# A gated dilated convolution on TensorE: seventeen six-step groups and three more short four-step groups in another order, in place of eighteen six-step groups

## The chip, the cores and the metric

The kernel runs on one core of one Trainium2 chip. A core has engines that run side by side and wait for each other by semaphores: TensorE (PE in the profile; PEld is its weight load), VectorE (DVE), ScalarE (ACT), GpSimd (POOL) and SyncE (SP, which here only issues DMAs). Matmul results lie in PSUM, everything else in SBUF. The metric is the device time of one execution in microseconds (us); lower is better.

## The reference

x has 2 sequences of 16,000 steps with 256 channels. A causal convolution with three taps, two steps apart, makes 512 channels; the first half goes through tanh, the second through a sigmoid, their product through a 256 x 256 matrix.

```python
B, T, D, K = (2, 16000, 256, 3)
dil = 2; pad = (K - 1) * dil
xp = jnp.pad(x, ((0, 0), (pad, 0), (0, 0)))
h = jnp.einsum('btc,cd->btd', xp[:, pad:pad + T, :], w[0])
for i in range(1, K):
    off = pad - i * dil
    h = h + jnp.einsum('btc,cd->btd', xp[:, off:off + T, :], w[i])
f, g = h[..., :D], h[..., D:]
z = jnp.tanh(f) * _sigmoid(g)
return z @ w_o
```

All data are bf16.

## The kernel before

**Fewer multiplications.** Steps are handled in groups. A group of kind B takes 4R successive steps and lays four of them beside each other; four products with transformed weights and inputs (m, p, d0, d3) replace the six that the taps would need. A group of kind A takes 6R steps and needs five products (by u1, rm, rp, r0, ri) where nine would be needed. R is 256 unless the table GROUPS says otherwise (B160 has R = 160). The first 640 steps (P160) are computed directly, by `direct`. So a product of kind A or B is a matmul of 2R columns, done for both halves of the channels (CT = 2, so always a pair), and one *block* is a group's products for one of four slices of 128 output channels (`oi` = 0 to 3).

**What each engine does for a block.** `product` issues TensorE's pairs: F (first), M (mid, kind A only), L (last), Z (zero), I (inf). `copy_first` (token c) has ScalarE copy the first product from PSUM to `ss`. `combine` (A, Y) and `second` (h; k is the same on ScalarE) are VectorE's sums over PSUM, tiles `a`, `yy` and `hh`; `activate` (b, y, a) is ScalarE's tanh or sigmoid, tiles `th` and `sg`. A block of kind A needs three of these sums (`hh`, `a`, `yy`), one of kind B only `a`. When both halves of a group's channels are done, `gate` (g) multiplies them on VectorE into `zz`, `out_mm` (P; H and R for the last group) applies w_o, and ScalarE or VectorE (tokens e and v, `out_evict`) moves the result to `osb`, from where SP stores it (s). Leftovers of R beyond a multiple of 128 go through `zo` and `odd`.

**The inputs of the products.** SP loads x transposed into `xt` (`load`, token x). `pre` makes the transformed inputs. Each may be made by VectorE in one instruction (128x1024, `u1.4`), by GpSimd in four quarters (128x256, tokens with q, as `u2.4q74`: the number tells behind which earlier VectorE instruction the quarter is held), or, for the second half of rp, rm, r0 and ri, by a DMA that adds one tile onto another in SBUF, issued from GpSimd's queue (tokens with d; rp lies in tile f, rm in e, r0 in u0, ri in u2, and the profile calls u0 to u3 all `u`). u3, uh and ud are scalings of u1. Tokens `wa` make one weight matrix on GpSimd at the start.

**What sets the order.** Nothing is scheduled by the compiler: ORDER lists the blocks by group number, and PLAN is one long list of tokens, each of which issues one instruction (or one pair or set of four matmuls). All engines run their own instructions in the order of that list. A and B blocks take their PSUM from two pools (`ps_b` with three banks, `ps_a` with two), output matmuls from `ps_o` with three.

Of the kernel before, what the change touches and what calls it, by code (L numbers as in the profile page):

```python
# [21 lines left out]
m.0 d3.0 p.0 F F d0.0 c F c G L w L A c D wa.5q2 D A wa.2q5 Z d0.1 I b D m.1 a L wa.3q1 F d A wa.10q2 Z c p.1 I  # L22
wa.6q1 b L a G Z wa.14q10 F A b x wa.4q7 I c g P a d3.1 F L u1.0 c wa.0q1 Z A I b wa.13q1 P e.0 a Z f.0 F b P g I x
c uh.0 L e0 m.2 L d3.2q1 a F A e1 P d3.2q2 A c Z u0.0 I b I u3.0 a r0.0d Z u2.0 L p.2 b x d3.2q1 F e2 A P e3 F ud.0
c d0.2 Z a I u1.1 c L b g P d3.2q1 a L A e4 F wa.12q14 A Z wa.8q30 c e.1 I b Z g a L u1.2 b F wa.1q1 P e5 A ri.0d F
c rp.0 I e6 rm.0 L c s3 Z u3.1 a s2 M uh.1 s0 b uh.2 I x u2.1 k0 P a A F wa.7q1 e7 L u0.1 wa.9q11 P c A Z e8 wa.11q6
M ud.1 wa.15q28 b I Y k1 F f.1 a Z f.2 c I b L g x M a A F k2 u2.2 P u1.3q14 c L Y e9 M u1.3q54 A y I k3 rp.1d u3.2
P Y a Z L g e10 Z b A f.3q36 P y ud.2 F f.3q28 b Y P c r0.1d rm.1 P y Z ri.1d e.2 e11 F e.3 I b rm.2d M g c F k4 M
u0.2 u0.3q1 a L h5 c I y A f.3q12 L a M f.3q62 Y e12 P A u1.3q8 e13 Z I Y k6 u1.3q43 I b g ri.2d L a rp.2d F u3.3 y
Z A rm.3d c P u1.4 b r0.2d P a Y M rp.3d F y uh.3 Z ud.3 k7 v15 I b L u3.4 e14 ud.4 F f.4q68 c A P c M u0.3q20 Y a M  # L30
e.4 k8 Z k9 g L rm.4d b I u0.3q33 A e17 P a v16 F f.4q36 L y Y s8 P f.4q55 c x A Z y u2.4q74 M Y b I e18 h10 Z a F g
b P c L u2.3 F e19 u1.5 ri.3d M c A I u0.3q60 k11 M Y a L u0.4 y f.4q1 P A k12 I Z e20 r0.3d uh.4 Y P a rp.4d L b
f.5 r0.4d Z y A F b I g c P u2.5q72 y F Y M e21 u3.5 u2.5q4 I c v22 P y u2.4q90 h13 Z a u2.4q16 v23 M b L u2.4q50
h14 a s10 P s9 e24 u2.5q44 A F x y L Y e.5q82 P c A e.5q79 Z e25 Y M e.5q58 y I h15 b e.5q69 Z a g ri.4d F e26 L c I
A f.6q22 b P s11 uh.5 M a u2.5q82 Y F y rp.5d u0.5 P k16 Z e.6 e27 r0.5d L b g I c P u2.6q118 A y F M e28 u1.6q63 Y
P c f.6q1 h17 Z y I ud.5 e29 rm.5 M b s12 L h18 a u2.6q1 x F a P u2.6q45 A c L Y u1.6q20 e30 I A u1.6q108 e31 M Z a
Y u1.6q33 P k19 g ri.5d Z b L e32 u0.6 P f.7q89 y A I b F uh.6 u2.6q46 e33 P Y c F r0.6d u3.6 P y g rm.6d M e34 I
f.6q13 a h20 P c Z y u1.7 L f.6q67 b M A e35 P rp.6d Y F k21 s14 P a e.7 s13 Z c ud.6 I g e36 ri.6d L b M u2.7q71 A
e37 P a h22 F u0.7q137 e38 P Y u0.7q65 c L s15 Z y uh.7 x u2.7q72 A M b I f.7q90 h23 e39 F f.7q1 y Y L c f.7q114 I
v40 a Z u2.7q22 Y a M g P b P k24 A F e41 x L rp.7 e42 P c A Z y u1.8 I u0.8q93 b M Y a P u0.7q161 h25 Z y F uh.8 b  # L40
u3.7 I u2.8 s16 c rm.7d F e43 f.8 M c L g rp.8d k26 M a u2.7q76 A L k27 Y I y u0.8q1 A Z a u0.7q103 P v44 b u0.8q81
L Y y s17 P u0.8q162 A e45 F r0.7d e46 Z ud.7 Y c I ri.7d P b u3.8 r0.8d M u1.9 a Z e.8 k28 F b ud.8 L rm.8d e.9 c I
y g F u2.9q179 M y A P c P e47 h29 f.9q46 M a Y s18 f.9q43 L e48 s1 ri.8 u2.9q60 Z x k30 I A b L u2.9q117 Y a F y
# [23 lines left out]
uh.17 p.3q67 Z e103 A M p.3q36 b s37 ud.17 I m.3q10 k67 Y P u0.17q286 a F v106 p.3q135 y L r0.17d Z c A P u2.17q16 y
M Y b I u2.17q30 e105 h68 Z a v107 F ri.17q5 b L ri.17q4 s38 y I A ri.17q3 P c Y F y ri.17q28 M c g Z a P h69 b P g
e108 M L e109 h70 F y I A c P a Y L I y Y Z a A M b P h71 y Z v110 F b L c I A F a L Y P c A I e113 v111 Z a L v112
Z b P A b s40 I g y s39 P a F I v114 c F P g c L a Z e115 A L P v116 b I e117 A Z s41 P g a s6 I b v118 Z a P b P  # L70
e119 g H P v120 s42 R P e121 H e123 v122 H R s44 R e124 s43 e125 s45
"""


# [572 lines left out]
```

## Time and profile before

| what | value |
|---|---|
| median of 3 runs | 258.78 us (258.61 to 259.19) |
| the profiled execution's own time | 258.77 us |
| its span, first to last instruction | 256.6 us |
| granted TensorE clock, mean | 0.995 |
| GpSimd's accumulating DMAs | 64 (18 + 16 + 15 + 15), 256 KB each |

The profile is of one execution; its span leaves out 2.2 us around the first and last instruction. A row of a group has the source line, engine, operation, output and input tiles with their shapes, a count, then the busy time, the mean duration in ns, and idle time before it with what ended that. A row of stretches has, after the stretch, each engine's busy time with a count. In the chain of work that ended last each piece has its start and its length, both in us, and what was running. Instructions that follow each other on one engine overlap a little, so the distance from start to start is the price of one more, and is less than its duration.

### The profile page before, as it was taken

To read this page: it belongs to the slowest core of one execution; us is meant where nothing else is said; L and a number is where in the kernel's file an instruction comes from. 1 tells how busy PE (TensorE), PEld (TensorE's weight loads), DVE (VectorE), ACT (ScalarE), POOL (GpSimd) and SP (SyncE) were. 2 spreads that over 40 slices of the span, in tenths; PEclk is the share of its full clock that TensorE was granted. 3 is DMA by queue.
4 is the path that set the end of the run, shared out by engine and by line. 5 is a ranking of instruction groups with operands and counts; after the bars stand their busy time and mean duration, and the time that the engine had idled before them with its cause. 6 is when DMAs were issued, how large, how long until landed. Compare 5 with 4: busy or idle time off the path is not lost.

```text
span 256.6 us, 4575 instructions
## 1 busy us (share of the span) xinstructions
PE 249.9 (97%) x1428; PEld 138.0 (54%) x1428; DVE 242.8 (95%) x405; ACT 243.7 (95%) x492; POOL 176.9 (69%) x249
## 2 busy tenths in 40 slices
PE   8999999999999999999999999999999999999992
PEld 4655555555555565545555555555555545555581
DVE  2999999999999999999999999999999999999991
ACT  4988999999999999999999999999999999999893
POOL 1064554997699888499764887999798798897000
PEclk9999999999999999999999999999999999999997
DMA  6999979989989899999999999996999998773054
GB/s 184 213 202 213 196 172 159 232 143 203 187 199 271 187 200 249 182 289 200 200 237 212 249 196 188 290 244 147 212 260 171 216 219 224 198 217 102 0 226 176
DMA packets 84320, 51.73 MB, mean 202 GB/s; under 512 B 69032, under 2 KB 70312, under 8 KB 84296
## 3 DMA queue, kind: packets, MB, share of 16 engines
q1 hardware_dynamic: 74168, 33.71, 54.3%
q0 software_dynamic: 9216, 16.78, 37.7%
q10 hardware_dynamic: 912, 0.95, 1.1%
q8 instruction: 11, 0.18, 0.3%
q14 instruction: 13, 0.11, 0.1%
HBM read 1.25 MB, written 16.38 MB: 69 GB/s over the span
## 4 chain that ended last, share of the span: by engine, by line
PE 82%; DVE 8%; DMA 3%; ACT 2%; issue 2%; ACTq 0%; DVEq 0%
PE b L359 48%; PE o_ps L478 18%; PE a L359 13%; DVE a L393 2%; DMA e<-u 2%; DVE zz L460 2%; DVE yy L393 2%; PE b L379 1%; PE a L379 1%; DMA xn<-in_x_dram 1%; DVE hh L393 1%; ACT osb L495 1%; ACT sg L441 1%; ACT th L441 0%; ACT ss L390 0%
## 5 line engine op out<-in xcount | busy, mean ns | idle before, releaser
L330 POOL TENSOR_TENSOR u<-xt 128x256 bf16<-128x256 bf16 x88 | 66.8, 774 | 15.0 <-PE b L359 8.4
L478 PE MATMUL o_ps<-wo_sb,zz 128*128 128x256 bf16 x496 | 72.0, 273 | 0.0
L495 ACT CAST osb<-o_ps 128x512 bf16<-128x512 f32 x101 | 63.8, 646 | 0.9 <-PE o_ps L478 0.7
L478 PEld LDWEIGHTS <-zz 128*128 128x128 bf16 x496 | 48.5, 98 | 27.6
L393 DVE SCALAR_TENSOR_TENSOR a<-ss,b 128x512 f32<-128x512 f32 (+1 forms) x88 | 59.5, 679 | 2.3 <-PE b L359 1.3
L390 ACT COPY ss<-b 128x512 f32<-128x512 f32 (+1 forms) x88 | 55.0, 628 | 0.9 <-PE b L359 0.6
L359 PEld LDWEIGHTS <-w_sb 128*128 128x128 bf16 x352 | 34.1, 97 | 35.1 <-issue 3.0
L359 PE MATMUL b<-e,wm_sb 128*128 128x512 bf16 x144 | 42.8, 379 | 0.3 <-DMA e<-u 0.3
L359 PE MATMUL b<-u,w_sb 128*128 128x512 bf16 x144 | 42.9, 379 | 0.2
L359 PE MATMUL b<-u,wa_sb 128*128 128x512 bf16 x144 | 42.9, 379 | 0.0
L359 PE MATMUL b<-f,wp_sb 128*128 128x512 bf16 x144 | 42.9, 379 | 0.0
L359 PE MATMUL a<-u,w_sb 128*128 128x512 bf16 x144 | 42.5, 379 | 0.3 <-DVE a L393 0.2
L460 DVE TENSOR_TENSOR zz<-th,sg 128x1536 bf16<-128x1536 bf16 (+2 forms) x46 | 41.3, 897 | 0.2
L441 ACT ACTIVATE th<-b 128x512 bf16<-128x512 f32 (+1 forms) x44 | 28.0, 636 | 1.4 <-ACT ss L390 0.7
L441 ACT ACTIVATE th<-a 128x512 bf16<-128x512 f32 (+1 forms) x44 | 28.6, 649 | 0.3 <-PE a L359 0.2
L441 ACT ACTIVATE sg<-b 128x512 bf16<-128x512 f32 (+1 forms) x44 | 28.0, 635 | 0.6 <-PE b L359 0.5
L441 ACT ACTIVATE sg<-a 128x512 bf16<-128x512 f32 (+1 forms) x44 | 28.3, 642 | 0.0
L359 PEld LDWEIGHTS <-wm_sb 128*128 128x128 bf16 x176 | 17.0, 98 | 17.2 <-DMA e<-u 1.2
L359 PEld LDWEIGHTS <-wp_sb 128*128 128x128 bf16 x176 | 16.9, 98 | 17.3 <-issue 1.6
L393 DVE SCALAR_TENSOR_TENSOR hh<-ss,b 128x512 f32<-128x512 f32 x38 | 25.9, 681 | 0.2
L393 DVE SCALAR_TENSOR_TENSOR yy<-hh,b 128x512 f32<-128x512 f32 x38 | 25.6, 678 | 0.0
L441 ACT ACTIVATE sg<-yy 128x512 bf16<-128x512 f32 x36 | 24.9, 693 | 0.7 <-DVE yy L393 0.7
(68 smaller groups left out, 373.2 us busy)
## 6 DMA issues: line engine op xcount, KB each, us to landing
out_dram<-osb SPq DMA_DIRECT2D x36, 384.0 KB, 3.5
u<-uh POOLq DMA_DIRECT2D x18, 256.0 KB, 4.8
f<-u POOLq DMA_DIRECT2D x16, 256.0 KB, 4.7
u<-ud POOLq DMA_DIRECT2D x15, 256.0 KB, 4.6
e<-u POOLq DMA_DIRECT2D x15, 256.0 KB, 4.8
out_dram<-osb SPq DMA_DIRECT2D x8, 256.0 KB, 3.1
w_sb<-in_w_dram ACTq DMA_DIRECT2D x3, 256.0 KB, 4.1
xt<-in_x_dram SPq DMA_TRANSPOSE x22, 8.0
```

Source lines behind the costliest of these rows:

```text
L330: ins = eng.tensor_tensor(out=o, in0=a, in1=b, op=op)
L359: nc.tensor.matmul(G[bank, oi][:, :2 * R], lhsT=wmat[:, ct, osl], rhs=G[mv][:, :, ct, :R], start=which == "first" and ct == 0, stop=ct == ...
L379: nc.tensor.matmul(G[bank, oi][:, :4 * r].rearrange("p (j r) -> p j r", j=4), lhsT=w_taps[tap][:, ct, osl], rhs=xt[:, j0:j0 + 4, ct, c0 + ...
L390: nc.scalar.copy(out=G["ss", oi][:, :n], in_=G["b", oi][:, :n])
L393: return note(nc.vector.scalar_tensor_tensor(out=out, in0=in0, scalar=scalar, in1=in1, op0=ALU.mult, op1=op))
L441: nc.scalar.activation(out=G[name, dt][:, j:j + 2, :R], in_=G[bank, oi][:, :2 * R].rearrange("p (q r) -> p q r", q=2), func=(ACT.Tanh, ACT ...
L460: note(nc.vector.tensor_tensor(out=G["z"][:, dt, :, :n], in0=G["th", dt][:, :, :n], in1=G["sg", dt][:, :, :n], op=ALU.mult))
L478: nc.tensor.matmul(o_ps[:, q, :], lhsT=z, rhs=wo_sb[:, dt, :], start=dt == 0 and (q == 0 or len(dts) == NT), stop=dt == NT - 1, skip_group ...
L495: copy(out=G["osb", at][:, 2 * jp:2 * jp + 2, :], in_=o_ps[:])
```

## The change

GROUPS, ORDER and PLAN are other tables; no function changes. The second sequence ends with a full B group and a B128 beside the B160, where it had one six-step group more. Group 21, a six-step group before, is now the full B group; one of its blocks stands inside each of the groups 1, 3, 5 and 7. One block of the B160 (22), which came last, stands inside or behind each of 12, 14, 16 and 18. The B128 (23) comes last.

```diff
 GROUPS = (
     "P160 A A A A A A A A B B B",
-    "A A A A A A A A A A B160",
+    "A A A A A A A A A B B160 B128",
 )
 ORDER = """
-9 9 9 9 10 10 10 10 11 11 11 11 1 1 1 1 2 2 2 2 3 3 3 3 4 4 4 4 5 5 5 5 6 6 6 6 7 7 7 7 8 8 8 8 12 12 12 12 13 13 13
-13 14 14 14 14 15 15 15 15 16 16 16 16 17 17 17 17 18 18 18 18 19 19 19 19 20 20 20 20 21 21 21 21 22 22 22 22
+9 9 9 9 10 10 10 10 11 11 11 11 1 21 1 1 1 2 2 2 2 3 21 3 3 3 4 4 4 4 5 5 21 5 5 6 6 6 6 7 7 21 7 7 8 8 8 8 12 12 12
+22 12 13 13 13 13 14 14 14 22 14 15 15 15 15 16 16 16 16 22 17 17 17 17 18 18 18 18 22 19 19 19 19 20 20 20 20 23 23
+23 23
 """
 PLAN = """
...
-e119 g H P v120 s42 R P e121 H e123 v122 H R s44 R e124 s43 e125 s45
+a P b P s44 e121 g P v122 H e123 H R R s45 e124 v125 s46
 """
```

Counted over both programs: TensorE has 40 products of 512 columns fewer, and 32 of 512 and 32 of 256 more. VectorE has two instructions fewer (fewer sums of 1024 columns, scalings, combinations and evictions, more short ones), ScalarE three more in all: six copies `hh` and four activations of `yy` fewer, four short copies and eight short activations more, two evictions `osb` more and one `odd` fewer. GpSimd has 172 sums in place of 160 and 62 accumulating DMAs in place of 64. SP loads and stores one piece more each. Since the two tables differ everywhere, three places show how rows move; lines of the changed kernel are higher by two.

VectorE before the change, where some 108 to 112 us of TensorE's work are done, up to the next gate (a, hh and yy are combinations, ud and u scalings, u, e and f on xt are inputs being made):

```order
L393 SCALAR_TENSOR_TENSOR yy<-hh,a 128x512
L393 SCALAR_TENSOR_TENSOR a<-ss,b 128x512
L328 TENSOR_SCALAR ud<-u_1406 128x1024
L393 SCALAR_TENSOR_TENSOR yy<-hh,a 128x512
L328 TENSOR_SCALAR u_1703<-u_1576 128x1024
L330 TENSOR_TENSOR u_1708<-xt 128x1024
L330 TENSOR_TENSOR e<-xt 128x1024
L328 TENSOR_SCALAR ud<-u_1576 128x1024
L330 TENSOR_TENSOR e<-xt 128x1024
L460 TENSOR_TENSOR zz<-th_1605,sg_1653 128x1536
```

Six of these ten rows prepare inputs. VectorE after the change, at 103 to 110 us of TensorE's work, from gate to gate:

```order
L462 TENSOR_TENSOR zz<-th_1495,sg_1565 128x1536
L395 SCALAR_TENSOR_TENSOR a<-ss,b 128x512
L395 SCALAR_TENSOR_TENSOR yy<-hh,a 128x512
L395 SCALAR_TENSOR_TENSOR hh<-ss,b 128x512
L332 TENSOR_TENSOR e<-xt 128x1024
L395 SCALAR_TENSOR_TENSOR a<-ss,b 128x512
L395 SCALAR_TENSOR_TENSOR yy<-hh,b 128x512
L395 SCALAR_TENSOR_TENSOR a<-ss,b 128x512
L395 SCALAR_TENSOR_TENSOR yy<-hh,a 128x512
L330 TENSOR_SCALAR ud<-u_1519 128x1024
L462 TENSOR_TENSOR zz<-th_1586,sg_1645 128x1536
```

Two rows between the gates prepare inputs; the others have moved to other places of VectorE's order, or to GpSimd.

GpSimd near its end, before the change, from the DMA that makes rp of the last six-step group (f) to the one that makes its rm (e):

```order
L325 DMA f<-u_3006 128x1024
L330 TENSOR_TENSOR u_3180<-xt 128x256
L330 TENSOR_TENSOR d_3084<-xt 128x160
L330 TENSOR_TENSOR u_3180<-xt 128x256
L330 TENSOR_TENSOR e<-xt 128x256
L325 DMA e<-u_3151 128x1024
```

The same, after the change (d_3153, d_3287 and p are inputs of the B128):

```order
L327 DMA f<-u_3001 128x1024
L332 TENSOR_TENSOR e<-xt 128x256
L332 TENSOR_TENSOR p<-xt 128x128
L332 TENSOR_TENSOR d_3287<-xt 128x128
L332 TENSOR_TENSOR p<-xt 128x128
L332 TENSOR_TENSOR d_3153<-xt 128x128
L327 DMA e<-u_3205 128x1024
```

Between e's last quarter and its DMA there are now four short sums for the last group.

TensorE in the first six-step group, before the change (w_sb, wm_sb, wp_sb and wa_sb are weights): behind the first group's mid product follows a product of the B group ahead of it.

```order
L359 LDWEIGHTS wm_sb
L359 MATMUL b<-e,wm_sb 128x512
L359 LDWEIGHTS wm_sb
L359 MATMUL b<-e,wm_sb 128x512
L359 LDWEIGHTS w_sb
L359 MATMUL a<-d_401,w_sb 128x512
L359 LDWEIGHTS w_sb
L359 MATMUL a<-d_401,w_sb 128x512
```

And after it: there the first product (m) of the added group 21 follows.

```order
L361 LDWEIGHTS wm_sb
L361 MATMUL b<-e,wm_sb 128x512
L361 LDWEIGHTS wm_sb
L361 MATMUL b<-e,wm_sb 128x512
L361 LDWEIGHTS wm_sb
L361 MATMUL b<-m,wm_sb 128x512
L361 LDWEIGHTS wm_sb
L361 MATMUL b<-m,wm_sb 128x512
```

The added group's products stand between those of the six-step group from the start of its first block on.

More of the change, by code (lines that the diff above doesn't have):

```diff
@@ L27 @@
[L27 to L31, printed above, removed]
@@ L67 @@
[L67 to L70, printed above, removed]
-e119 g H P v120 s42 R P e121 H e123 v122 H R s44 R e124 s43 e125 s45
+m.0 d0.0 p.0 F F d3.0 c F c G L w L A c D wa.4q3 D A D wa.12q4 Z d3.1 d Z b m.1 I b F d0.1 L G c I p.1 a wa.0q1 L a
@@ new lines @@
+F A wa.3q7 P A c x wa.8q2 P e0 u2.0 Z I f.0 b L u1.0 a P Z e1 g wa.5q1 I b A F a F rp.0 c I g c Z x u0.0 L b P p.2
+e2 wa.2q1 L a A F e3 wa.6q21 P A c wa.14q21 Z m.2 I x b d3.2 L a F ud.0 u3.0 Z c uh.0 P u1.1 b wa.7q1 I e4 A L
+wa.10q12 a F d0.2 wa.1q29 e5 Z A I c wa.11q3 P b g r0.0d Z a e.0 F b I f.1 c rm.0d L g a F ri.0d A L rp.1d c P m.3
+e6 Z e.1 I s3 b s0 L A wa.13q1 a s2 F u3.1 e7 e.2q5 x Z A c I u0.1 b Z M d0.3 a F g k0 P b p.3 L c I uh.1 e.2q1 e8 A
+F a L wa.9q13 Y P c e.2q42 A y Z wa.15q46 M u1.2 rm.1d b Z d3.3 k1 F x e9 u2.1 I c L u0.2 a P u3.2 M b A I k2 g F
@@ new lines @@
+e.2q1 a L Y c P ud.1 e10 u2.2q1 Z A M b r0.1d uh.2 I ud.2 k3 ri.1d F Y a L f.2 c Z f.3q62 A y I M b u2.2q55 Y P e11
+rm.2d u1.3 F y Z rp.2d h4 c I b g M u2.3q46 e12 L h5 a F s6 y P Y x f.3q62 L c A u2.3q41 P a Y u2.2q68 Z e13 I A y
+u2.3q57 M b g u2.2q46 Z a F h6 b I c uh.3 P ri.2d ud.3 y F u3.3 r0.2d s5 M e14 e.3 L c u0.3 rm.3d P k7 Y P f.3q43 a
+L A e15 M y A u2.3q82 I e16 Z h8 f.3q85 a P Y r0.3d L b u1.4 rp.3d Z e17 F A ri.3d b I g c F u2.4q27 a L Y c I A y Z
+u2.4q7 M a v18 u2.4q84 Z b h9 P y ud.4 F b u0.4 L c f.4 F e19 M g c P k10 I A e20 M Y a L s9 e.5q96 I k11 s4 A
@@ new lines @@
+u2.4q82 Z x a L Y e.5q86 b P A y Z u1.5 e21 F I b Y P c u3.4 F a e.4 M c g Z rm.4d x k12 M g b I y L h13 u2.5q45 P
+e22 A F a u2.5q81 L y Y u2.5q107 P c Y Z f.5q17 y M A u2.5q58 b I h14 e23 rp.4d I uh.4 a Z s8 g L r0.4d y F b e.5q44
+A P e24 ri.4d Y F c P u3.5 a Z u1.6 c M u0.5 b I e.6q33 h15 M y F a g e.6q11 L k16 P c A L e25 f.5q5 Y M e26 e.5q44
+I A k17 Z s11 uh.5 a P s10 u3.6 x b L ud.5 Y P e27 ri.5q40 F e28 A e.6q1 Z c Y I f.5q128 b L r0.5 rm.5d a I y
+f.5q116 F A Z e29 uh.6 P c rp.5d ud.6 s12 Z b u2.6 x M e30 g P a F b u0.6 P u1.7q42 c P h18 y F f.6 ri.5q131 M e31 L
@@ new lines @@
+f.12q83 k42 Z g a rp.11d Z b L rm.11d u1.12 b P ri.11d A y F F r0.11d c u3.12 I e71 Y L c P u2.12 a Z u0.12 y I A M
+b u1.13 P a e.13q35 Z h43 y I F g b e.12q45 L e72 F c A s27 P a s26 e.12q15 Y M c s7 I f.12q15 e73 h44 M e74 ud.12 L
+k45 ud.13 ri.12d Z e75 Y L f.13q25 a A s28 P b s20 P A e.12q71 y Z Y e76 f.13q25 F I b u3.13 rm.12d Z g c rp.12d F
+uh.12 b u0.13 M r0.12d c P g k46 M a L u2.13 e.14q225 k47 I A e77 F u1.14 a L e.14q102 P c Y P y f.13q102 A M e78
+e.13q34 Z Y e79 s29 P f.13q88 b h48 x I y e.13q202 Z v80 a L e.13q104 v81 F b g I c P u2.14q153 y A F a M rm.13d
@@ new lines @@
+u3.14 c Y P rp.13d e82 I h49 M y uh.13 Z k50 g r0.13d L b P ri.13d Y e83 L u2.14q92 a F A e84 P A Z c s31 f.14q44 P
+Y e85 s1 I u2.14q108 b s30 M x u0.14 f.14q145 a F Z h51 c I y e.14q41 v86 L b ud.14 P a Y f.15q130 F y A e.14q168 P
+c L uh.14 f.14q37 Z y A I b u1.15 f.14q259 M a I h52 Z e87 e.15q22 F b L g e.15q121 c F a x M A c P e.15q291 k53 Y M
+e89 f.15q203 v88 L k54 Z u2.14q265 A y I e.15q96 b L Y P y rp.14d g F a rm.14d Z e90 A ri.14d I c P r0.14d Y b P y
+v91 M e92 P u1.16 Z a h55 P b u3.15 F e93 g L rm.15d c I s34 f.15q157 A y F s33 s32 M Y c u0.15q274 I h56 a Z
@@ L72 @@
+L a u2.16 Z r0.16d y M ud.16 A b P ri.16q10 I k64 Y ri.16q31 F y v105 Z a m.5q26 g L p.5q32 y P b A I ri.16q5 c P Y
+e106 F ri.16q108 e107 M v108 m.5q43 Z c m.5q22 h65 s39 P a s36 M b s38 g L k66 I e109 Y F a L A y P A c P I y Y Z M
+b Z h67 e110 P a v111 F s40 L v112 c I b A P a Y L F y I A c v113 Z a P g b L Z y P A b F v114 I c I g Z e115 s42 F
+L a s41 P a A c P b P e116 g L e117 v118 I Z P s43 A b P e119 I v120 Z a P a b P s44 e121 g P v122 H e123 H R R s45
+e124 v125 s46
 """
```

60 lines of the change are left out of this document (20 added, 40 removed).

## The prediction

> **What bounds the kernel.** I read first the page's busy times, then the chain of work that ended last, cut into three stretches, because a mean over 256.6 us hides which engine leads where.
>
> ```profile
> PE 249.9 (97%) x1428; PEld 138.0 (54%) x1428; DVE 242.8 (95%) x405; ACT 243.7 (95%) x492; POOL 176.9 (69%) x249
> by line: PE b L359 60.6%; PE o_ps L478 21.0%; PE a L359 16.0%; DVE zz L460 1.1%; DVE a L393 0.9%; DVE yy L393 0.8%; issue 0.1%
> ...
> by line: PE b L359 40.8%; PE o_ps L478 14.6%; PE a L359 11.0%; DVE zz L460 6.1%; DVE yy L393 5.9%; DVE a L393 5.7%; DVE hh L393 4.5%; issue 4.5%; DVE f L330 1.8%; DVE u L330 1.4%; DVE u L328 1.1%; ACT th L441 1.0%; DVE osb L487 0.8%; DVE uh
> ...
> by line: PE b L359 51.4%; PE o_ps L478 19.6%; PE a L359 13.1%; DMA e<-u 6.7%; ACT sg L441 1.9%; ACT osb L495 1.8%; DVE a L393 1.6%; issue 1.4%; ACT ss L390 1.3%; ACT th L441 0.8%; DVE yy L393 0.5%; DVE uh L328 0.4%
> ```
>
> The first row says that TensorE, VectorE and ScalarE are all full. The next three are the chain from 20 to 100 us, 100 to 160 us and 160 to 240 us. TensorE alone carries the first (97.6%) and most of the third (84%); in the second its lines make 66.4% and VectorE's named lines 27.3%. So the kernel is bound by TensorE, except between 100 and 160 us, where VectorE leads.
>
> How much TensorE loses there I get from its own pace. The rows below are, in turn: four chain pieces; the timeline's first six-step or four-step products; three groups by shape (five rows such as the first have x144, four such as the second x24); and the products (L359) and output matmuls (L478) in two stretches.
>
> ```profile
> 144.88 0.86 PE b L359 x4
> ...
> 247.31 0.27 PE a L359 x2
> ...
> 248.84 2.63 PE o_ps L478 x24
> 251.47 0.02 issue
> ...
> 11.30 1.46 PE L359 MATMUL b<-m,wm_sb 128*128 128x512 bf16 x6
> ...
> L359 PE MATMUL b<-u,wa_sb 128*128 128x512 bf16 x144 | 42.9, 379 | 0.0
> ...
> L359 PE MATMUL b<-p,wp_sb 128*128 128x512 bf16 x24 | 6.9, 379 | 0.0
> ...
> L478 PE MATMUL o_ps<-wo_sb,zz 128*128 128x256 bf16 x496 | 72.0, 273 | 0.0
> ...
> 60.00:100.00 40.00, 33.61 (x138) 1.00 0.99 213
> 100.00:160.00 60.00, 50.48 (x209) 1.00 1.09 218
> ...
> 60.00:100.00 40.00, 13.80 (x92) 1.00 0.99 213
> 100.00:160.00 60.00, 17.20 (x120) 1.00 1.09 218
> ```
>
> A 512-column matmul takes 0.86/4 = 0.215 us when nothing holds it, a 256-column one 2.63/24 = 0.1096 us, a 320-column one 0.27/2 = 0.135 us; the means of 379 and 273 ns are pipelined durations. From 11.30 to 251.47 us, 240.2 us pass. The work in them is 816 x 0.215 (five times 144 and four times 24) + 500 x 0.1096 (four odd ones are added to the 496) + about 38 x 0.135 = 235.3 us. So TensorE idles about 4.9 us in all. In 100 to 160 us it is 60 - 209 x 0.215 - 120 x 0.1096 = 1.9 us, in 60 to 100 us 40 - 138 x 0.215 - 92 x 0.1096 = 0.25 us; a pair that straddles an edge is counted too, so up to 0.4 us more each. That is 0.03 us of idling per us where VectorE leads and about 0.01 to 0.02 elsewhere.
>
> **The change, part by part.**
>
> *TensorE gains work.* One six-step group (40 products of 512 columns) becomes a four-step group (32 of 512) and a short one (32 of 256): 32 x 0.110 - 8 x 0.215 = +1.8 us. The 256-column product has no row; I take the output matmul's, of equal width. Its bounds are half a 512-column product, 0.108, and the 320-column 0.135, so +1.7 to +2.6 us. The output matmuls keep their number. TensorE carries the chain outside one stretch, so nothing hides this.
>
> *VectorE loses work.* Its chain at the worst place gives the spacings, which are shorter than the durations since instructions overlap:
>
> ```profile
> 107.54 0.68 DVE hh L393
> 108.23 0.34 DVE uh L328
> 108.56 0.34 DVE u L328
> 108.90 0.60 DVE u L330
> 109.50 0.61 DVE f L330
> 110.11 0.87 DVE zz L460
> 110.97 0.62 DVE a L393
> 111.63 0.59 PE a L359 x2
> ...
> L393 DVE SCALAR_TENSOR_TENSOR a<-ss,b 128x320 f32<-128x320 f32 x4 | 2.0, 488 | 0.0
> ...
> L460 DVE TENSOR_TENSOR zz<-th,sg 128x512 bf16<-128x512 bf16 x4 | 1.7, 417 | 0.0
> ```
>
> Eight VectorE instructions stand in a row here, and a product waits behind the last of them. By kind: net three fewer 1024-column sums (-1.8 us), three fewer scalings (-1.0), two fewer 512-column combinations (-1.2), two 1536-column gates fewer and two of 1024 more (-0.5), two evictions fewer (-1.2); against these one 640-column sum (+0.4), four 256-column combinations (at most 0.40 by the 320-column row less the 0.08 overlap, so +1.3 to 1.6), two short gates (+0.7) and one short eviction (+0.3). Sum about -2.9 us. ScalarE loses six copies for the combinations and gains narrow activations, as the rows of its kinds price them:
>
> ```profile
> L403 ACT COPY hh<-b 128x512 f32<-128x512 f32 x34 | 21.3, 632 | 0.0
> ...
> L441 ACT ACTIVATE th<-yy 128x512 bf16<-128x512 f32 x36 | 25.1, 698 | 0.0
> ...
> L441 ACT ACTIVATE th<-a 128x320 bf16<-128x320 f32 x2 | 0.9, 446 | 0.0
> ...
> L495 ACT CAST osb<-o_ps 128x512 bf16<-128x512 f32 x101 | 63.8, 646 | 0.9 <-PE o_ps L478 0.7
> ```
>
> -6 x 0.63 - 4 x 0.70 + 2 x 0.65 + 12 narrow ones at 0.37 to 0.44 (0.44 is the 320-column row; 0.37 an estimate by width from 698 and 446) - 0.4 for an odd eviction = -0.4 to -1.3 us. Neither counts in full: they lie beside TensorE, and pay only as far as TensorE waited for them.
>
> *How that spreads decides.* I cut both orders at each 20 us of TensorE work and price what VectorE has beside it at the spacings above. Before, from 20 to 220 us: 19.8, 19.6, 20.7, 18.3, 21.1, 20.5, 20.1, 18.9, 19.3, 19.4. After: 20.1, 20.2, 19.8, 19.0, 19.3, 19.1, 18.9, 20.1, 18.4, 17.9. The overload of 1.7 us between 100 and 160, where 1.9 to 2.3 us are lost, is gone; a new one of 0.3 us stands between 20 and 60, and a small one at 160 to 180. So the middle stretch falls to the common rate, 60 x 0.015 = 0.9 us, a gain of 1.2; 20 to 60 gets 0.3 worse, 160 to 180 0.2 worse, and lighter ScalarE and a lighter end give back some 0.5. Net: idling from 4.9 to 3.7 us, -1.2. Bounds: it stays at 4.9 (as many products as before stand just one pair behind the VectorE or ScalarE instruction that they need: 22 and 68 before, 19 and 70 after, and a pair is 0.43 us against 0.6 to 0.7 for the instruction), or falls to 2.0 (all at the rate of 60 to 100 us, 0.25 in 40 us, and DMA waits as now).
>
> *GpSimd and its DMAs.* Twelve quarters more and two DMAs fewer; the queue is busy for 69%, so its sum costs nothing, but its lateness may.
>
> ```profile
> L330 POOL TENSOR_TENSOR u<-xt 128x256 bf16<-128x256 bf16 x88 | 66.8, 774 | 15.0 <-PE b L359 8.4 <-PE a L359 4.0 <-DVE e L330 1.1
> ...
> e<-u POOLq DMA_DIRECT2D x15, 256.0 KB, 4.8
> ...
> 201.43 0.87 POOL L325 DMA_DIRECT2D e<-u  x1
> ...
> 202.02 1.43 POOL L325 DMA_DIRECT2D f<-u  x1
> ...
> 205.88 0.59 PE L359 MATMUL b<-u,w_sb 128*128 128x512 bf16 x2
> ...
> 206.81 0.61 PE L359 MATMUL b<-e,wm_sb 128*128 128x512 bf16 x2 [0.34 <-DMA e<-u]
> ```
>
> The accumulating DMA of e issued at 201.43 is waited for until 206.81; the pair before it began at 205.88 and needed 0.43, so 0.5 us are lost. In the order 4.3 us of TensorE work stand between the two. After, the closest such pair (e of the last six-step group) has 3.9 us, and three others near it 4.3 to 4.8; before, the tightest had 4.3, three times, and one of these waited. I count the same 0.6 us of DMA waits as now, with 0 and 1.5 (each of three late by 0.5) as the ends.
>
> The Trainium skill, "DMA: Bandwidth & Descriptors", section "Anatomy of one DMA — SWDGE (gpsimd) path", puts such a DMA at 2.0 us plus its bytes at 436 GB/s: an estimate of 2.6 us for 256 KB. By that none of these products would wait and the time would be 0.6 us lower. The trace disagrees, with a median of 4.8 us to landing.
>
> *Loads, stores and the ends.* One load of x becomes two and one store is added on SP's queue; no piece of the chain is a load of x, so I cost that at zero; if one came late, VectorE's sums over it would, and the products behind them. The lead-in starts with the same three B groups; I cost it at zero, covered by TensorE's own work. At the end both last evictions were ScalarE's, one behind the other; after, the last is VectorE's:
>
> ```profile
> 251.49 1.07 ACT L495 CAST osb<-o_ps 128x512 bf16<-128x512 f32 x2 [0.34 <-PE o_ps L478]
> ```
>
> 1.07 us for two becomes some 0.9 (the second matmul group ends 0.22 later, and 0.69 for one): -0.15 us, and no less than 0.
>
> Sum: +1.8 - 1.2 - 0.15 = +0.45 us on the profiled execution's 258.77 us (span 256.6), which is also the median of the runs, 258.78. Forecast **259.2 us**. About 0.2%, 0.5 us, is what a measurement of this kernel can tell from no change.
>
> **Rivals.**
> 1. *VectorE's relief goes further (faster).* For it: the middle stretch loses 0.03 us per us, 60 to 100 us only 0.006. Against: two stretches now carry 20.1 and 20.2. Idling 2.0: 258.77 + 1.8 - 2.9 - 0.15 = 257.5. It beats no change once more than 1.65 us of idling go.
> 2. *The close pairs decide, not the load (slower).* For it: 89 close pairs as against 90, on a TensorE with 1.8 us more to do. Against: of the VectorE ones those outside 100 to 160 us cost little. Idling unchanged: 260.4.
> 3. *GpSimd late.* In the stretch 120 to 130 us of TensorE work fourteen quarters and three DMAs stand, at 0.774 a quarter and 0.59 an issue (201.43 to 202.02) up to 12.6 us for 10, and the last quarter of an operand m stands 1.3 us ahead of its product; then the DMA with 3.9. One wait of 0.5 to 1.0 more on top of the forecast: 259.7 to 260.2.
> 4. *TensorE is not the bound at all.* If its matmuls had room, the added products would vanish and VectorE's 2.9 us would count: 255.9. Against: matmuls at 0.215 without a gap for 97.6% of a chain. In this sense reads the Trainium skill, "Perfetto Trace Analysis", section "Identifying the Most-Contended Engine": matmul busy time misleads, weight loads' busy share tells the headroom. That share is 54% here, against 97%, and the trace disagrees with that reading.
>
> **Chances.** Forecast with idling of 3.1 to 4.3 (258.6 to 259.8) 0.42, rival 1 0.25, rival 2 0.18, rival 3 0.12, rival 4 0.03. Faster than 258.3: nearly all of rivals 1 and 4, 0.27. Slower than 259.3: rivals 2 and 3 and a quarter of the forecast's own weight, 0.40. Between: 0.33. The range goes from 257.4, a little below rival 1, to 260.8, rival 2 with half of what a dearer narrow product could add; likelier than its ends is 258.6 to 259.8.
>
> **What would show it.** In the trace after: matmul counts of 136 and 32 in place of 144 and 24, and eight groups of x8 with 256 columns at 0.11 spacing; VectorE's share of the chain in 100 to 160 us well below 27%, and some VectorE in 20 to 60; TensorE's idling by the same count near 3.7 us; VectorE's busy time down by about 2.9 us; no wait for GpSimd above 0.3 us near 140 us, and a DMA wait of about 0.5 us between 220 and 235. The prediction is wrong if idling stays at 4.9 or falls below 2.5, or if the narrow products don't keep pace.

## The result: slower by 0.9%, and the profile after

The changed kernel takes 261.38 us (median of 8 runs, 259.66 to 261.85), the kernel before on the same chip 258.95; the ratio is 1.0086, 95% interval 1.0066 to 1.0105. The forecast was 259.2 us with a range up to 260.8. The profiled execution after took 261.18 us, its span is 259.4 us.

The page's busy times, and then the chain of work that ended last from 100 to 160 us and from 160 to 240 us, all of the changed kernel:

```profile
PE 251.3 (97%) x1452; PEld 140.4 (54%) x1452; DVE 242.6 (94%) x403; ACT 244.0 (94%) x495; POOL 182.3 (70%) x259
...
by line: PE b L361 54.3%; PE o_ps L480 21.8%; PE a L361 13.6%; DVE a L395 2.2%; ACT th L443 1.8%; ACT sg L443 1.7%; DVE yy L395 1.5%; DVE hh L395 1.1%; DVE zz L462 1.0%; DVE uh L330 0.9%; issue 0.4%; DVEq L395 0.1%; DVEq L332 0.0%
...
by line: PE b L361 56.5%; PE o_ps L480 19.1%; PE a L361 13.7%; DMA f<-u 6.7%; DVE hh L395 0.9%; DVE a L395 0.9%; DVE yy L395 0.7%; POOL e L332 0.7%; DVE ud L330 0.6%; issue 0.4%; DVEq L395 0.1%
```

In the middle stretch TensorE's lines went from 66.4% to 89.7% and VectorE's from 27.3% to 6.7%: the stretch that VectorE led is TensorE's now, as forecast. But VectorE's busy time fell by 0.2 us only, not by 2.9. In the last stretch the wait for one accumulating DMA has 6.7% again, on f in place of e.

TensorE's idling, added up from each matmul that starts later than its predecessor's pace allows, was 5.2 us before (4.9 by the forecast's subtraction) and is 7.0 us after. From 100 to 160 us it fell from 2.3 to 1.3 us; from 180 to 200 us it rose from 0.1 to 1.8, from 220 to 240 us from 0.3 to 1.5. Two rows of TensorE's timeline carry most of that rise:

```profile
185.28 0.59 PE L361 MATMUL b<-f,wp_sb 128*128 128x512 bf16 x2 [0.80 <-DVE hh L395]
...
225.11 0.59 PE L361 MATMUL b<-f,wp_sb 128*128 128x512 bf16 x2 [1.08 <-DMA f<-u]
```

The brackets count from the modelled end of the matmul before; by pace the two stops are 0.96 and 1.25 us. The chain's piece ahead of the second (start, us, what):

```profile
219.60 5.38 DMA f<-u
```

At 225 us a product waits for rp of the sixteenth six-step group, whose DMA was issued at 219.60 us and landed 5.38 us later. The product also has to come behind VectorE's hh, which ends at 224.17 us, 0.3 us after the product could have started, so the DMA alone costs some 0.9 us of the 1.25. At 185 us VectorE's hh is late. The timeline of GpSimd (POOL) and VectorE a few microseconds earlier shows why:

```profile
178.45 1.21 POOL L327 DMA_DIRECT2D u<-uh  x1
179.50 1.95 POOL L332 TENSOR_TENSOR e<-xt 128x256 bf16<-128x256 bf16 x2
181.42 0.66 POOL L332 TENSOR_TENSOR f<-xt 128x256 bf16<-128x256 bf16 x1
...
178.08 0.68 DVE L332 TENSOR_TENSOR u<-xt 128x1024 bf16<-128x1024 bf16 x1
179.55 1.37 DVE L332 TENSOR_TENSOR u<-xt 128x1024 bf16<-128x1024 bf16 x1
180.84 0.68 DVE L395 SCALAR_TENSOR_TENSOR a<-ss,b 128x512 f32<-128x512 f32 x1
181.44 1.19 DVE L332 TENSOR_TENSOR u<-xt 128x1024 bf16<-128x1024 bf16 x1
```

The same sum takes 0.68 us alone and 1.37 and 1.19 us while GpSimd sums quarters out of the same memory; the combination between them, which reads PSUM, keeps its 0.68. And the accumulating DMAs take longer to land than the 4.6 to 4.8 us of before:

```profile
e<-u POOLq DMA_DIRECT2D x17, 256.0 KB, 4.9
u<-uh POOLq DMA_DIRECT2D x16, 256.0 KB, 5.2
f<-u POOLq DMA_DIRECT2D x15, 256.0 KB, 5.4
u<-ud POOLq DMA_DIRECT2D x14, 256.0 KB, 5.7
```

So two explanations stood against each other: late DMAs, and VectorE made late by GpSimd's quarters. A third was that the forecast's own terms were wrong.

### The profile page after: what moved, and what is told of

It reads as the page before. It is cut to its first block, busy times and chain, and to the rows that moved or that the text cites. A ratio compares the mean times of both kernels' runs of the same rounds, so it can differ in the third digit from the quotient of the medians.

```text
span 259.4 us, 4599 instructions
## 1 busy us (share of the span) xinstructions
PE 251.3 (97%) x1452; PEld 140.4 (54%) x1452; DVE 242.6 (94%) x403; ACT 244.0 (94%) x495; POOL 182.3 (70%) x259
## 3 DMA queue, kind: packets, MB, share of 16 engines
HBM read 1.25 MB, written 16.38 MB: 68 GB/s over the span
## 4 chain that ended last, share of the span: by engine, by line
PE 88%; DMA 3%; DVE 3%; ACT 3%; issue 1%; POOL 0%; DVEq 0%
PE b L361 52%; PE o_ps L480 19%; PE a L361 14%; DMA f<-u 2%; PE b L381 1%; DMA xn<-in_x_dram 1%; PE a L381 1%; ACT sg L443 1%; DVE a L395 1%; DVE hh L395 1%; ACT th L443 1%; DVE yy L395 1%; ACT ss L392 0%; ACT osb L497 0%; PE tp L244 0%
## 5 line engine op out<-in xcount | busy, mean ns | idle before, releaser
L395 DVE SCALAR_TENSOR_TENSOR a<-ss,b 128x512 f32<-128x512 f32 (+2 forms) x92 | 60.8, 666 | 2.3 <-PE b L361 1.3
L392 ACT COPY ss<-b 128x512 f32<-128x512 f32 (+2 forms) x92 | 55.2, 603 | 4.2 <-PE b L361 3.9
L332 POOL TENSOR_TENSOR u<-xt 128x256 bf16<-128x256 bf16 x60 | 46.0, 778 | 8.1 <-PE a L361 3.0
L361 PE MATMUL b<-f,wp_sb 128*128 128x512 bf16 x136 | 40.4, 379 | 2.2 <-DMA f<-u 1.1
L361 PE MATMUL b<-u,w_sb 128*128 128x512 bf16 x136 | 40.3, 378 | 0.3 <-DVE a L395 0.2
L332 POOL TENSOR_TENSOR e<-xt 128x256 bf16<-128x256 bf16 x40 | 32.0, 805 | 11.8 <-PE b L361 5.1
L443 ACT ACTIVATE sg<-b 128x512 bf16<-128x512 f32 (+2 forms) x46 | 28.3, 616 | 1.3 <-PE b L361 1.0
L443 ACT ACTIVATE th<-b 128x512 bf16<-128x512 f32 (+2 forms) x46 | 28.2, 612 | 0.6 <-PE b L361 0.4
L443 ACT ACTIVATE sg<-a 128x512 bf16<-128x512 f32 (+2 forms) x46 | 28.6, 621 | 0.0
L443 ACT ACTIVATE th<-a 128x512 bf16<-128x512 f32 (+2 forms) x46 | 28.4, 617 | 0.0
```

What stands on the lines that cost most here:

```text
L332: ins = eng.tensor_tensor(out=o, in0=a, in1=b, op=op)
L361: nc.tensor.matmul(G[bank, oi][:, :2 * R], lhsT=wmat[:, ct, osl], rhs=G[mv][:, :, ct, :R], start=which == "first" and ct == 0, stop=ct == ...
L392: nc.scalar.copy(out=G["ss", oi][:, :n], in_=G["b", oi][:, :n])
L395: return note(nc.vector.scalar_tensor_tensor(out=out, in0=in0, scalar=scalar, in1=in1, op0=ALU.mult, op1=op))
L443: nc.scalar.activation(out=G[name, dt][:, j:j + 2, :R], in_=G[bank, oi][:, :2 * R].rearrange("p (q r) -> p q r", q=2), func=(ACT.Tanh, ACT ...
```

## Experiments: taking single waits away

All edits are to PLAN, the written order; the numbers behind q are left out here. `rp.15d` is the accumulating DMA that is waited for at 225 us, `e.14q` a quarter of e, `u2.13` and `u1.14` VectorE's two stretched sums.

**The late DMA issued earlier.**

```
-... e95 Z y u0.15q M Y b ... e97 Z rp.15d Y L ...
+... e95 Z y u0.15q rp.15d M Y b ... e97 Z Y L ...
```

> The changed kernel with one DMA earlier in GpSimd's order: the one that makes rp of the second last six-step group stands six quarters sooner. Theory A (the DMA is issued too late; TensorE lost 1.25 us at 225 us waiting for it): the wait goes, the time falls by 1.0 to 1.25 us, to about 260.1 us, ratio to the kernel before 1.0045. Rival (the wait covers another that comes due at the same place, so nothing is won): 261.2 us, ratio 1.0086, and TensorE stops within 2 us of the same place.

Measured 260.80 us, 1.0082 of before (1.0064 to 1.0100). The wait at 225 us is gone, and the idling from 220 to 240 us falls from 1.46 to 0.54 us; from 200 to 220 us it rises from 0.44 to 0.81. The time's interval overlaps the changed kernel's.

**Three close DMAs earlier** (`rp.8d` and `rm.12d` too, by 10 and 9 tokens).

> The changed kernel with all three late DMAs earlier (rp of the 9th, rm of the 13th, rp of the 16th six-step group; TensorE lost 0.46, 0.18 and 1.25 us at them). Theory A: 1.6 to 1.9 us less than the changed kernel, about 259.5 us, ratio 1.002. Rival (waits move on to the next late DMA or to VectorE): not below 260.5 us, ratio 1.006 or more.

Measured 262.96 us, 1.0163 (1.0147 to 1.0180): slower than the changed kernel. The timeline of this run:

```profile
180.06 2.16 DVE L462 TENSOR_TENSOR zz<-th,sg 128x1536 bf16<-128x1536 bf16 x1
180.40 2.35 POOL L332 TENSOR_TENSOR e<-xt 128x256 bf16<-128x256 bf16 x2
182.15 1.15 DVE L332 TENSOR_TENSOR u<-xt 128x1024 bf16<-128x1024 bf16 x1
182.28 0.94 PE L480 MATMUL o_ps<-wo_sb,zz 128*128 128x256 bf16 x7 [0.56 <-DVE zz L462]
```

With the issues moved, GpSimd's quarters fall beside the gate zz, 0.95 us when alone and 2.16 here, and an output matmul waits for it.

**The quarters held back** behind VectorE's sum `u1.14`, alone and with the three DMAs earlier.

```
-... L u2.13 e.14q k47 I A e77 F u1.14 a L e.14q ...
+... L u2.13 k47 I A e77 F u1.14 e.14q a L e.14q ...
```

> The changed kernel with one GpSimd quarter held back behind the VectorE sum u1 of the 15th six-step group, so that VectorE's two sums at 179.5 and 181.4 us run without GpSimd. Theory B (GpSimd's quarters stretched these two sums from 0.69 to 1.37 and 1.19 us and so made VectorE late by 1.2 us, which TensorE lost at 182 to 186 us): both sums last 0.69 us, 0.8 to 1.1 us less, about 260.3 us, ratio 1.005. Rival (VectorE was late for its own load, or the quarters stretch other VectorE work instead): within 0.3 us of the changed kernel, ratio 1.0075 to 1.0095.

> The three earlier DMAs and the held quarter together. Theories A and B: they add up, 2.5 to 2.9 us less than the changed kernel, about 258.5 us, ratio 0.997 to 1.0: the added TensorE work of 1.8 us would be paid for by the VectorE load taken away. Rivals: what one wait gives back the next takes, 260 us or more, ratio 1.004 or more.

Measured 261.36 us, 1.0105 (1.0085 to 1.0125), and 261.61 us, 1.0115 (1.0093 to 1.0137). In the first the two sums last 0.68 us again and the wait at 185 us is gone. A gate 7 us on takes their place:

```profile
185.84 2.02 POOL L332 TENSOR_TENSOR e<-xt 128x256 bf16<-128x256 bf16 x2
186.14 1.18 DVE L462 TENSOR_TENSOR zz<-th,sg 128x1536 bf16<-128x1536 bf16 x1
```

In the second the two sums last 0.68 us too, but the small product `zo` ahead of them takes 1.37 us, where it takes 0.21 alone, and the wait at 185 us is as long as before:

```profile
177.66 1.37 DVE L458 TENSOR_TENSOR zo<-th,sg 128x128 bf16<-128x128 bf16 x1
...
185.64 0.59 PE L361 MATMUL b<-f,wp_sb 128*128 128x512 bf16 x2 [0.79 <-DVE hh L395]
```

**Quarters given to VectorE**: e of one group made by one VectorE sum in place of four quarters (`e.14q` four times becomes `e.14` once, at 195 us); then e of two groups, with `rp.15d` early.

> The changed kernel with input e of the 15th six-step group made by VectorE in one instruction near 200 us, where VectorE has the least work, instead of four GpSimd quarters, two of which met VectorE's sums at 179.5 and 181.4 us. Theory B (these meetings cost TensorE 1.2 us at 182 to 186 us): 0.6 to 1.1 us less than the changed kernel, ratio 1.004 to 1.006. Rival (the next quarters in GpSimd's order take their place and meet the same sums): no less, ratio 1.0075 or more.

> The changed kernel with inputs e of the 15th and of the 17th six-step group on VectorE (eight GpSimd quarters fewer between 175 and 235 us), and the DMA for rp of the 16th issued earlier. Theory (GpSimd's lateness and its meetings with VectorE are what was lost): 1.6 to 2.2 us less than the changed kernel, about 259.3 us, ratio 1.001 to 1.003. Rival (VectorE, now with 1.2 us more work, or another wait takes it): ratio 1.006 or more.

Measured 262.17 us, 1.0111 (1.0083 to 1.0140), and 261.89 us, 1.0110 (1.0078 to 1.0142). No gain. In both, the wait at 185 us is as long as before; the first waits for VectorE three times from 180 to 200 us, where the changed kernel waited twice.

```profile
183.92 0.59 PE L359 MATMUL a<-u,w_sb 128*128 128x512 bf16 x2 [0.55 <-DVE yy L393]
185.92 0.59 PE L359 MATMUL b<-f,wp_sb 128*128 128x512 bf16 x2 [0.80 <-DVE hh L393]
...
198.36 0.59 PE L359 MATMUL b<-u,w_sb 128*128 128x512 bf16 x2 [0.79 <-DVE a L393]
```

**VectorE's two sums later**, alone and with `rp.15d` early.

```
-... a L u2.13 e.14q k47 I A e77 F u1.14 a L ... Z v80 a L ... I c P u2.14q ...
+... a L e.14q k47 I A e77 F a L ... Z v80 u2.13 a L ... I c P u1.14 u2.14q ...
```

> The changed kernel with two of VectorE's sums over x (the u of the two six-step groups next in line, the ones that ended at 180.9 and 182.6 us) put 7 and 10 us later in its order, ahead of their first readers still. By the theory that VectorE's clump of sums beside GpSimd's quarters is what is late at 182 to 198 us, the idling of TensorE between 180 and 200 us falls from 1.79 to about 0.6 us and the time from 261.4 to about 260.2 us. By the theory that VectorE is as full as TensorE over the whole last third, so that work put later is late later, the 180 to 200 us window falls and the 200 to 220 us one rises by about as much, and the time stays at 261.0 to 261.8 us.

> Both that and the accumulating DMA for rp of the sixteenth six-step group issued about 3 us earlier, which by itself took the wait at 225 us away. If the two waits (1.2 and 1.1 us) are separate causes, the time falls by both, to about 259.2 us, near the kernel before. If each wait taken away comes back nearby, 260.5 to 261.8 us.

Measured 260.76 us, 1.0090 (1.0074 to 1.0106), and 260.87 us, 1.0087 (1.0072 to 1.0102). The idling from 180 to 200 us is 1.86 and 1.84 us, as it was: the wait stands 3.5 us later, behind the moved sum, which is stretched there.

```profile
186.94 1.15 DVE L331 TENSOR_TENSOR u<-xt 128x1024 bf16<-128x1024 bf16 x1
188.75 0.59 PE L360 MATMUL a<-u,w_sb 128*128 128x512 bf16 x2 [0.75 <-DVE a L394]
```

Eight edits, and none brings the kernel measurably nearer to the one before. The DMA wait at 225 us goes in each trace in which that DMA is earlier; the wait for VectorE at 185 us goes in one, and elsewhere stays or moves by a few microseconds. Where a wait goes, others come within some 20 us. In every trace that has the wait at 185 us some VectorE instruction is stretched by 0.5 us or more shortly before, and in those without it none is; which one it is depends on the run. Moving single meetings didn't help.

## Experiments: taking whole terms away

**TensorE's added work.** The products of the short group use one of two contraction halves.

```
-        for ct in range(CT):
+        cts = range(CT) if R > P else range(1)
+        for ct in cts:
...
-                start=which == "first" and ct == 0, stop=ct == CT - 1, skip_group_check=True,
+                start=which == "first" and ct == 0, stop=ct == cts[-1], skip_group_check=True,
```

> The changed kernel, in which the products of the short group (128 rows) use one of their two contraction halves: 16 of its 32 products of 256 columns are left out, nothing else is. By the forecast's first term TensorE sets the end there, so the time falls by the work left out, 16 x 0.1096 = 1.75 us, from 261.4 to 259.6 us, and the chain's last stretch stays TensorE's. The rival is that ScalarE, VectorE or the output matmuls behind them set the end of the kernel: then the idling between the short group's matmuls grows by what is left out, and the time stays within 0.5 us of 261.4.

Measured 259.98 us, 1.0060 (1.0035 to 1.0084). Against 1.0086 the drop is 0.7 us by the ratios, with some 0.8 us of uncertainty, and 1.4 by the medians, of the 1.75 left out. The rest is idling near the end, where it rose from 0.03 to 0.96 us: with less work TensorE waits for VectorE and ScalarE there.

```profile
248.50 0.27 PE L362 MATMUL a<-d,w_sb 128*128 128x256 bf16 x1 [0.23 <-DVE a L396]
```

So at least a part of the added work is probably paid; the ratios can't say how much of it.

This trace shows something else. Up to the last group its program is that of the changed kernel, but in this execution GpSimd's quarters are stretched near 181 us and not VectorE's two sums:

```profile
180.71 2.46 POOL L332 TENSOR_TENSOR e<-xt 128x256 bf16<-128x256 bf16 x2
...
180.76 0.68 DVE L332 TENSOR_TENSOR u<-xt 128x1024 bf16<-128x1024 bf16 x1
...
181.96 0.68 DVE L332 TENSOR_TENSOR u<-xt 128x1024 bf16<-128x1024 bf16 x1
...
185.31 0.59 PE L362 MATMUL b<-f,wp_sb 128*128 128x512 bf16 x2
...
197.16 0.59 PE L362 MATMUL b<-u,w_sb 128*128 128x512 bf16 x2 [0.21 <-DVE a L396]
```

There is no wait at 185 us, and the idling from 180 to 200 us is 0.75 us in place of 1.79; from 60 to 100 us it is 0.99 in place of 0.43. The short wait at 197 us is there all the same. So which meeting costs how much differs between executions of the same order, and the size of a single wait in one trace holds for that execution.

**GpSimd's reading**: each of its quarters becomes a fill with zeros, in both kernels, and once more on another chip.

```
-        if op is None:
+        if eng is nc.gpsimd:
+            ins = eng.memset(o, 0.0)
+        elif op is None:
```

> The kernel before, with every GpSimd quarter that prepares an input replaced by a fill with zeros of the same place: the sums are left out, GpSimd reads nothing and is done sooner; all order and all waits stay. Theory (GpSimd's quarters stretch VectorE's sums and delay the DMAs, a little here): 0.4 to 1.2 us less than the kernel before, ratio 0.995 to 0.999. Rival (GpSimd costs nothing, TensorE and VectorE alone decide): ratio 0.999 to 1.001.

> The changed kernel with the same replacement: every GpSimd quarter that prepares an input is a fill with zeros, so the sums are left out. Theory (what is lost against the forecast is GpSimd's: stretched VectorE sums at 180 us and late DMAs): 2.5 to 3.2 us less than the changed kernel, about 258.5 us, ratio 0.996 to 1.001, and within 0.8 us of the kernel before with the same replacement. Rival (the added TensorE work and products close behind their VectorE sums decide): 260.5 us or more, ratio 1.006 or more, and 2 us above the kernel before with the replacement.

> The changed kernel in which every operand quarter on GpSimd is a fill with zeros instead of a sum of two parts of x (the sums are left out), once more on another chip: the first time the DMAs on that chip came late by 2 to 4 us. By the theory that GpSimd's reading beside VectorE costs the time, the stretched VectorE sums go (the 1.37 and 1.19 us ones last 0.69) and the time falls by 1.2 us or more, to 260.2 us or below. By the theory that what counts is when the accumulating DMAs come in, the sums go to 0.69 us all the same and the time stays at 261 us or goes above it, with waits for DMAs in the place of the stretched sums.

Measured 1.0021 (0.9997 to 1.0045) for the kernel before, 1.0160 (1.0115 to 1.0205) and 1.0197 (1.0164 to 1.0231) for the changed one. The stretched sums and gates are gone (none lasts over 0.08 us longer than its median), and the changed kernel is slower all the same. The trace kept of it is of the fastest of its six executions (261.48 us; the others took 263.7 to 266.5). Of four DMAs issued there from 160.6 to 162.5 us three take 11.7 to 13.2 us to land, where four issued as close in the changed kernel (164.9 to 166.5 us) took 5.7 to 7.9; why is open. And the fills hold VectorE in another way:

```profile
211.63 2.26 DVE L332 TENSOR_SCALAR uh<-u 128x1024 bf16<-128x1024 bf16 x1
212.00 0.30 POOL L330 MEMSET e<- 128x256 bf16 x1
212.25 0.56 POOL L330 MEMSET u<- 128x256 bf16 x2
...
213.31 0.30 POOL L330 MEMSET e<- 128x256 bf16 x1
...
215.13 0.59 PE L363 MATMUL b<-u,w_sb 128*128 128x512 bf16 x2 [1.38 <-DVE yy L397]
```

A scaling of 0.42 us lasts 2.26 us, to the end of an unbroken row of fills, and TensorE waits 1.38 us behind it. So this pair doesn't take the interference away. By their times the rivals came (1.006 or more; 261 us or above), but the fills have a part in that which neither had named.

**No accumulating DMAs, with the quarters and with fills**, in both kernels.

```
-            return settle(nc.gpsimd.dma_start(out=G[name][:, :, :, :R], in_=b, accum_op=op), False)
+            return None
```

> The kernel before without its 64 accumulating DMAs on GpSimd's queue (the operand that each would complete is used as it is; the sums are left out). Its TensorE waits for them 0.6 us in all, so 258.8 becomes about 258.2 us if that is all they cost. It stands as the base of the next run.

> The changed kernel without its 62 accumulating DMAs, in the same way; GpSimd's quarters stay. If late DMAs are what the forecast missed, the distance to the kernel before, 2.4 us, shrinks here to the forecast's own terms, 0.5 to 1.2 us: about 259.2 us. If GpSimd's quarters beside VectorE's sums are what it missed, the distance stays at 2 to 2.5 us: 260.3 to 261 us. If only TensorE's added work counts, it is 1.3 to 1.8 us: 259.5 to 260 us.

> The kernel before without its accumulating DMAs, and with GpSimd's quarters turned into fills with zeros (both sums are left out): neither late DMAs nor stretched sums can hold TensorE. VectorE's own load between 100 and 160 us is left: 257.2 to 258.2 us.

> The changed kernel treated alike. What is left of the distance to the run before is TensorE's 1.8 us, less the idling of 1.0 to 1.2 us that VectorE's relief between 100 and 160 us gives back and less 0.2 to 0.5 us at the end: +0.1 to +0.6 us. If the forecast's terms were wrong themselves, and not what was added to them, +1.8 us or more stays.

| GpSimd's queue has | before, us and ratio | after, us and ratio | after against before |
|---|---|---|---|
| quarters and DMAs | 258.95, 1 | 261.38, 1.0086 | +0.86% |
| fills and DMAs | 1.0021 (0.9997 to 1.0045) | 1.0160 (1.0115 to 1.0205) | +1.39% |
| quarters alone | 263.16, 1.0171 | 262.59, 1.0154 | -0.17% |
| fills alone | 256.54, 0.9921 (0.9909 to 0.9933) | 256.68, 0.9926 (0.9913 to 0.9939) | +0.05% |

The last row decides between the queue and the forecast's own terms. With neither late DMAs nor reading quarters, the change costs 0.1 us, give or take 0.5, where the forecast's sum said 0.45. No change would fit as well; the 2.4 us of the kernels as they are would not. The chain from 100 to 160 us (the view itself cuts the row's tail) and the busy times, first of the kernel before, then of the changed one, both with fills alone:

```profile
by line: PE b L361 46.6%; PE o_ps L480 17.5%; PE a L361 11.8%; DVE zz L462 2.9%; ACT ss L392 2.8%; ACT th L443 2.6%; ACT osb L497 2.4%; DVE hh L395 2.3%; ACT sg L443 2.0%; DVE a L395 2.0%; DVE yy L395 1.8%; issue 1.7%; DVE u L330 1.1%; DVE 
...
PE 249.1 (98%) x1428; PEld 138.2 (54%) x1428; DVE 239.8 (94%) x405; ACT 243.3 (95%) x492; POOL 53.2 (21%) x185
```

```profile
by line: PE b L363 60.2%; PE o_ps L482 25.5%; PE a L363 14.8%
...
PE 249.4 (98%) x1452; PEld 140.5 (55%) x1452; DVE 238.4 (94%) x403; ACT 243.4 (96%) x495; POOL 54.5 (21%) x197
```

TensorE's idling is 3.9 us in the one and 2.7 in the other: the forecast's -1.2. TensorE's last matmul starts 0.27 us later all the same (at 250.17 and 250.44), which leaves some 1.5 us for its added work. VectorE's busy time falls by 1.4.

Quarters alone cost more than quarters and DMAs together: the kernel before gets 4.5 us slower when its DMAs are left out. More of VectorE's work then meets the quarters: its stretched instructions last 9.7 us longer than their medians in all, against 4.1 with the DMAs. That the DMAs' issues otherwise hold the quarters up is a guess. Its timeline shows such meetings, and its busy times behind that:

```profile
92.51 0.66 POOL L330 TENSOR_TENSOR u<-xt 128x256 bf16<-128x256 bf16 x1
92.54 0.92 DVE L328 TENSOR_SCALAR uh<-u 128x1024 bf16<-128x1024 bf16 x1
...
95.20 3.34 POOL L330 TENSOR_TENSOR u<-xt 128x256 bf16<-128x256 bf16 x4 [0.58 <-PE a L359]
96.29 1.14 DVE L330 TENSOR_TENSOR u<-xt 128x1024 bf16<-128x1024 bf16 x1
96.42 0.59 PE L359 MATMUL b<-f,wp_sb 128*128 128x512 bf16 x2 [0.43 <-DVE hh L393]
```

```profile
PE 251.5 (96%) x1428; PEld 137.8 (53%) x1428; DVE 247.9 (95%) x405; ACT 244.8 (94%) x492; POOL 127.5 (49%) x185
```

VectorE has 247.9 us for the work that takes it 239.8 beside fills.

For the row with quarters alone the three theories had the distance at 0.5 to 1.2 us, 2 to 2.5, or 1.3 to 1.8. It came out at -0.6, outside all three, and the kernel before at 263.16 us where 258.2 was expected. With fills alone that kernel came out below its 257.2 to 258.2, the distance inside its 0.1 to 0.6. Read together, the four rows say one thing more: the distance is there in both rows with DMAs and in neither without. That speaks for the DMAs, but is no proof, since in the row with fills the fills themselves held VectorE up, and quarters alone slow both kernels by more than the distance.

## Why the prediction was wrong, step by step

The step that failed is TensorE's idling: it was to fall by 1.2 us, from 4.9 to 3.7, and it rose by 1.8, from 5.2 to 7.0 by the finer count. The forecast had named idling that stays at 4.9 as a sign of being wrong. Term by term:

- **TensorE's added work, +1.8 us: right in mechanism, some 1.5 us by the last pair and 1.7 by the kernels as they are.** The chain after has the narrow products at half pace, 0.44/4 and 0.22/2 = 0.11 us:

```profile
248.57 0.44 PE a L361 x4
...
250.97 0.22 PE b L361 x2
```

- **VectorE's relief between 100 and 160 us, -1.2 us of idling: right.** 2.3 to 1.3 us in the kernel as it is (0.46 of what is left is a DMA wait), 3.9 to 2.7 us over the whole span in the last pair (-1.6 of it from 100 to 160 us, so that the sum is nearer than its parts). The finer terms were near too: 160 to 180 us +0.25 (forecast +0.2); 20 to 60 us hardly changed, +0.05 (forecast +0.3).
- **VectorE's work, -2.9 us: right in size, but its busy time was the wrong place to look.** Added up one by one, VectorE's durations fall by 3.2 us in the last pair (271.1 to 267.8) and by 2.5 in the kernels as they are (273.5 to 271.0), where GpSimd's quarters stretch some. The page's busy time counts overlapping instructions once. After the change VectorE stops more often (46 times in place of 30, and 54 in place of 37 in the last pair), fewer of its instructions overlap, and the busy time falls by 0.2 and 1.4 us only. The forecast's "eight" in a row are seven in its lines; no sum uses that.
- **"I count the same 0.6 us of DMA waits as now, with 0 and 1.5 as the ends": the first cause of the failure.** They are 0.46 + 0.18 + 1.25 = 1.9 us, some 0.3 of which VectorE would have cost alone. The longest wait came on rp of the sixteenth six-step group, whose lead in the order is 4.3 us; the DMA with the least lead, 3.9 us, landed in 3.3 us and was not waited for. A lead in the order doesn't rank them, since landing took from 3.3 to 7.9 us. The trace of before had the same spread, 3.3 to 7.7.
- **No term at all for GpSimd's quarters beside VectorE: the second failure.** The wait at 185 us cost 0.96 us, and is absent from the traces in which nothing of VectorE's is stretched shortly before (the held quarter alone, and the halved products). The 0.36 us at 197 us stay in both, so the stretched sums don't cause them. The trace of before held stretched gates of up to 1.45 us, and the forecast priced VectorE by medians.
- **The end, -0.15 us: -0.6.** From the start of TensorE's last matmul to the end of the span 5.2 us became 4.6. The time outside the span fell too, from 2.2 to 1.8 us, which the forecast didn't look at and no run explains.

Put together, from the two traces: work +1.69, idling +1.76, end -0.60, outside the span -0.44, in all +2.41 us (258.77 to 261.18). Idling is thus 3.0 us from its forecast: 1.3 by DMA waits, 1.3 by VectorE late at 185 and 197 us, the rest in small pieces. These sizes are one execution's. Rival 3, GpSimd late, had the nearest mechanism; it looked near 140 us and at the last group, and had 0.12.

Shown is that the loss beyond the forecast's terms comes from GpSimd's queue: with its sums and DMAs out of both kernels the distance is +0.05%, with them +0.86%. How much of it is the DMAs' and how much the quarters' stays open: either one without the other is slower than both, or no faster, so neither can be taken away by itself with the rest unchanged. Why the changed order suffers more, 1.6% against 0.8%, is argued only: it has twelve quarters more and two DMAs fewer, and its sums and gates stand at other places of the order. No experiment beats the kernel before with the whole computation in it.

## What to carry to other kernels

An engine's load counted at undisturbed durations came out too low here, where a second engine works in the same memory: read the longest of a group beside its median, and give the difference a term of its own. In an order packed this tightly, moving one DMA or one sum moves the collision and seldom removes it; test a whole term (all DMAs, all helper sums) in both kernels before blaming one wait, and look for that wait in a second trace of the same order. And a DMA's time to land is a spread, not a figure: rank waits by issue, landing and first use in the trace.

## Unexpected of the hardware

- VectorE's instructions out of SBUF stretch beside GpSimd's sums: a 128x1024 sum from 0.68 to 1.37 us, a 128x1536 gate from 0.95 to 2.16, a 128x1024 scaling from 0.42 to 0.92, a 128x128 product from 0.21 to 1.37. In these rows the extra is 0.5 to 1.2 us and doesn't grow with the instruction's length. Combinations that read PSUM kept 0.67 to 0.70 us. The other side pays too: two quarters in a row took 1.95, 2.35 and 2.46 us, against 1.30 undisturbed.
- GpSimd's fills leave VectorE's two-input sums alone, but hold a one-input scaling up: 2.26 us in place of 0.42, until the row of fills ended.
- Accumulating DMAs of 256 KB landed in 3.3 us at best. Four issued within 2 us took 5.7 to 7.9 us in the changed kernel, and up to 13.2 in the one with fills.
